# Which engine waits for the output store: GpSimd or ScalarE

## The chip, the cores and the metric

The kernel runs on one core of one Trainium2 chip. The profile of the core lists the instructions of TensorE (PE; PEld is its weight load), VectorE (DVE), ScalarE (ACT), GpSimd (POOL) and SyncE (SP), 10032 in all in the kernel before, and gives the DMA's time as a share of 16 engines. In this kernel the engines' programs meet through semaphores. The metric is the device time of one execution in microseconds (us), the median of several executions.

Two kinds of evidence are used:

- times of whole executions, which for one kernel in one set of rounds spread by 0.06 to 0.8 us;
- the trace's own records, to the nanosecond: the instructions, the updates of each semaphore, and the DMA packets. The semaphore records go on after the kernel's last instruction, in the kernel before from 0.122 to 2.269 us after the store's last increment, so they also show how the core leaves the program. All times "after the last increment" below are taken from these records; tables in plain fences were made from them.

The "span" is the time from the kernel's first instruction to its last in the profile; the reported time is longer (1287.31 against 1285.28 us in the profiled run of the kernel before), as it also holds what the core does on leaving.

## The reference, cut to what matters

The reference is one decode step for one token: attention over a cache of 32768 keys for 32 heads, plus a SwiGLU feed-forward block, plus the input. Its result is one row of 640 bfloat16 values.

```python
x = A_x
xn = _layernorm(x, axis=-1)
return x + _A_ref(xn, A_k_cache, A_v_cache, A_wq, A_wo) \
         + _B_ref(xn, B_w_gate, B_w_up, B_w_down)
```

The caches make the work: 554 MB come from HBM, 1280 bytes go back. Only the way those 1280 bytes are waited for is at issue here.

## The kernel before: the parts that matter

`nc.Block` gives each engine a program. SyncE issues all the large loads and, at the very end, the store of the result:

```python
@block.sync
def sp(e):
    ...                                   # all loads
    e.wait_ge(s_fin, 2)                   # VectorE has cast the output row
    e.dma_start(out[0, 0:1, :].rearrange("o (r m) -> (o r) m", m=32),
                orow[:, :]).then_inc(s_out, 16)
```

`then_inc(s_out, 16)` is the program's request that the store's completion raise the semaphore `s_out` to 16. In the trace of the kernel before, that semaphore has eleven records after the store's issue, from 0.498 to 1.259 us after it. An engine waits until it stands at 16; the wait is meant to keep the program from ending before the result has landed. Every version measured here has such a wait, and no run tests what happens without one. Before the change it is GpSimd, which otherwise only builds constants at the start (its last memset ends at 4.5 us):

```python
@block.gpsimd
def pool(g):
    def done(ins):
        ins.then_inc(s_const, 1)
        n[0] += 1
        g.wait_ge(s_const, n[0])
    ...                                   # identity matrices, masks
    for a in range(RB):
        done(g.memset(blk[a * 32:(a + 1) * 32, a:a + 1], 1.0))
    assert n[0] == 6 + 2 * RB
    g.wait_ge(s_out, 16)
```

ScalarE's last work lies well before the end (it ends at 1270.33 us):

```python
@block.scalar
def act(a):
    ...
    a.wait_ge(s_f, 1)
    a.activation(out=sg[:, 0, :], in_=ffn[:, 0:FB], func=ACTF.Exp, scale=-1.0).then_inc(s_fa, 1)
```

Two details of the surroundings matter. The kernel empties its last block (`nc.main_func.blocks[-1].instructions = []`), and its engines end one by one: in the changed kernel GpSimd's final branch starts at 4.5 us and ScalarE's at 1284.8 us. And in these traces a wait is carried by the instruction behind it. `done` leaves a wait for `s_const` pending after the last memset, and GpSimd's last two records in the kernel before are one instruction that only waits for `s_out` (17 ns), then a compare-and-branch that carries the wait for `s_const` (32 ns). The profile gives that branch the line of the `with` statement, L80. An engine with nothing pending shows no such branch: in the kernel before L80 has one record, GpSimd's, in the changed kernel two, GpSimd's and ScalarE's.

## Time and profile before

| | before |
|---|---|
| time, median of 3 runs (range) | 1286.85 us (1286.80 to 1286.95) |
| span of the profiled run | 1285.3 us |
| HBM traffic, rate | 554 MB, 431 GB/s |
| SyncE issues the output store | 1283.903 us |
| last completion increment of the store | 1285.162 us |
| GpSimd's final branch ends; the span ends with it | 1285.284 us |

Lines of the page of the kernel before: its span, the DMA share in 40 slices, and the main DMA queue.

```profile
span 1285.3 us, 10032 instructions
...
DMA  9999999999999999999999999999999999999998
...
q1 hardware_dynamic: 10974, 554.00, 99.7%
...
HBM read 553.99 MB, written 0.00 MB: 431 GB/s over the span
```

The DMA engines are at least 90% busy in every slice but the last, and the main queue's packets take 99.7% of the span at 431 GB/s: by these figures the kernel is bound by HBM traffic. The view by stretches of time shows where that stops. The columns are the stretch, its length, the busy time of each engine, the granted TensorE clock, the share of DMA and GB/s.

```profile
core 0: us, PE busy (x) PEld busy (x) DVE busy (x) ACT busy (x) POOL busy (x), PEclk, DMA share, GB/s
1252.00:1270.00 18.00, 17.63 (x413) 17.50 (x412) 2.52 (x6) 1.14 (x4) 0.00 (x0) 0.59 0.99 418
1270.00:1282.00 12.00, 6.20 (x207) 5.87 (x204) 0.96 (x5) 0.18 (x1) 0.00 (x0) 0.50 0.94 385
1282.00:1285.30 3.30, 1.39 (x37) 1.12 (x34) 0.36 (x2) 0.00 (x0) 0.00 (x0) 0.50 0.03 8
```

After 1282 us the DMA share is 0.03. These last 3.3 us are a chain of short instructions, each waiting for the one before, and, with a DMA share of 0.94 to 0.99 in the two stretches before, the one in which half a microsecond on GpSimd or ScalarE can count. The timeline of this stretch, before (start, length, engine, line, operation):

```profile
1283.22 0.18 DVE L641 TENSOR_TENSOR outb<-ps,blk 128x20 bf16<-128x20 f32 x1 [11.79 <-PE ps L451]
...
1283.46 0.20 PE L476 MATMUL ps<-fold,outb 128*20 128x32 bf16 x1 [0.27 <-DVE outb L641]
1283.70 0.18 DVE L644 CAST orow<-ps 20x32 bf16<-20x32 f32 x1 [0.29 <-PE ps L476]
1283.90 0.39 SPq L255 DMA_DIRECT2D out_dram<-orow  x1
```

The timeline ends with the store, but the span ends 1 us later: waits and branches are not drawn there. The view of single source lines shows them, first GpSimd's wait for the store:

```profile
L278 POOLq EVENT_SEMAPHORE  x1: 17/17/17, 1285.2 to 1285.2; - x1
```

and then the branch behind it:

```profile
L80 POOLq COMPARE_BRANCH  x1: 32/32/32, 1285.3 to 1285.3; - x1
```

Each line gives the count, the length in ns and the first and last start in us. In the trace they start at 1285.186 and 1285.252 us.

What happens then is in no view of the profile, only in the semaphore records. In the kernel before, semaphore 2 is raised step by step ("ticks"), nine times up to 1025 ns after the last increment. From 945 to 1591 ns 245 semaphores have one record each, in five groups by number of 47 to 50 (46 to 51 in the changed kernel), which I read as resets. From 1905 to 2269 ns nine more ticks follow. I read the first nine ticks as a barrier, and the last nine as a second one; no view names them. I call the first five ticks, one by each engine (the experiments with each engine in turn as the last show which is whose), the way out, and the next four the way back; a step from one tick to the next is a hop. The "exit" of an engine is the time from the end of its final branch to its own tick. In ns after the store's last increment:

```
                     barrier, way out              way back            last barrier
kernel before   -1326 -1292  747  791  814    906  944  978 1025    1905 ... 2269
                          ^ GpSimd's branch ended at 122
```

Two engines had long ticked. The third tick comes 747 - 122 = 625 ns after GpSimd's branch, and the rest follows.

### The profile page before, as it was taken

How to read it: one execution, taken by the hardware profiler on the slowest of the kernel's cores; microseconds unless marked ns; L12 is line 12 of the kernel's file. 1: busy time of each engine (PE TensorE's matmuls, PEld its weight loads, DVE VectorE, ACT ScalarE, POOL GpSimd, SP SyncE). 2: the span in 40 equal slices, each digit the busy share in tenths (PEclk: the TensorE clock that was granted, in tenths of full speed). 3: DMA queues.
4: the chain of work that ended last, by engine and by line, in shares of the span. 5: the costliest groups of instructions: out<-in, count | busy, mean ns of one | idle time of the engine just before them, and what ended most of it. 6: DMA issues, size and time to landing. Idle time of an engine off the chain costs nothing.

```text
span 1285.3 us, 10032 instructions
## 1 busy us (share of the span) xinstructions
PE 1041.2 (81%) x5160; PEld 261.3 (20%) x3240; DVE 672.3 (52%) x409; ACT 52.1 (4%) x139; POOL 2.6 (0%) x18
## 2 busy tenths in 40 slices
PE   3599777789788789778898877798787798778797
PEld 1022112221112221112221112221112221112227
DVE  0855665445665446664446664446654446654441
ACT  2000000000000000000000000000000000000000
POOL 0000000000000000000000000000000000000000
PEclk9799888898888898888998888898888998888995
DMA  9999999999999999999999999999999999999998
GB/s 424 424 447 429 428 437 435 428 432 439 432 432 432 439 428 432 439 432 432 428 443 428 432 439 432 432 426 445 428 432 439 430 434 426 441 432 432 439 419 364
DMA packets 10987, 554.16 MB, mean 431 GB/s; under 512 B 1247, under 2 KB 1504, under 8 KB 1760
## 3 DMA queue, kind: packets, MB, share of 16 engines
q1 hardware_dynamic: 10974, 554.00, 99.7%
q8 instruction: 9, 0.15, 0.0%
q14 instruction: 2, 0.02, 0.0%
q10 hardware_dynamic: 2, 0.00, 0.0%
HBM read 553.99 MB, written 0.00 MB: 431 GB/s over the span
## 4 chain that ended last, share of the span: by engine, by line
DMA 53%; PE 28%; DVE 12%; issue 6%; DVEq 0%; SPq 0%
DMA ring<-in_A_k_cache_dram 51%; PE ps L358 16%; DVE ring L577 12%; PE ps L310 9%; DMA ring<-in_A_wo_dram 2%; PE ps L342 1%; PE ps L329 1%; PE ps L400 0%; PE ps L394 0%; PE ps L388 0%; PE ps L451 0%; SPq L252 0%; DVEq L577 0%; DVE sc L583 0%; DVE pmax L589 0%
## 5 line engine op out<-in xcount | busy, mean ns | idle before, releaser
L577 DVE TENSOR_TENSOR ring<-ring,qb 128x8192 bf16<-128x8192 bf16 x128 | 557.8, 4421 | 315.8 <-DMA ring<-in_A_k_cache_dram 315.8
L310 PE MATMUL ps<-ring,ident 128*128 128x512 bf16 x1920 | 497.2, 418 | 0.0
L358 PE MATMUL ps<-ring,P 128*4 128x512 bf16 x1920 | 429.0, 379 | 0.0
L329 PE MATMUL ps<-ring,ident 128*128 128x512 bf16 x128 | 55.9, 437 | 220.1 <-DVE ring L577 219.8
L358 PEld LDWEIGHTS ps<-ring,P 128*4 128x4 bf16 x1920 | 158.1, 85 | 230.1
L329 PEld LDWEIGHTS ps<-ring,ident 128*128 128x128 bf16 x128 | 12.6, 98 | 617.6 <-issue 309.7
L583 DVE TENSOR_REDUCE sc<-ps 128x64 f32<-128x512 f32 x128 | 82.3, 686 | 62.8 <-PE ps L310 62.8
L595 DVE TENSOR_SCALAR negb<-ps 128x1 f32<-128x1 f32 x32 | 5.1, 159 | 108.4 <-PE ps L400 108.4
L503 ACT ACTIVATE P<-sc,negb 128x256 bf16<-128x256 f32 x32 | 16.2, 508 | 956.9 <-DVE negb L595 956.9
L592 DVE TENSOR_REDUCE m<-ps 1x1 f32<-1x128 f32 x32 | 8.9, 278 | 85.2 <-PE ps L394 85.2
L380 PEld LDWEIGHTS ps<-identf,o 4*128 4x128 f32 x248 | 30.7, 190 | 13.1 <-issue 13.1
L380 PE MATMUL ps<-identf,o 4*128 4x1 f32 x248 | 33.3, 251 | 0.0
L388 PEld LDWEIGHTS ps<-rsum,ones 128*128 128x128 f32 x64 | 12.1, 190 | 99.3 <-issue 98.5
L494 ACT ACTIVATE o<-ps,rzb 4x512 f32<-4x512 f32 x31 | 21.0, 677 | 6.3 <-PE ps L345 6.3
L301 PE MATMUL ps<-ring 128*128 x40 | 10.6, 432 | 11.2 <-DMA ring<-in_A_wq_dram 11.2
L499 ACT ACTIVATE ocol<-ps 128x1 f32 (+1 forms) x31 | 5.4, 173 | 222.4 <-PE ps L380 222.4
L342 PE MATMUL ps<-ring,P 128*4 x64 | 14.4, 379 | 0.0
L589 DVE TENSOR_REDUCE pmax<-sc 128x1 f32<-128x256 f32 x32 | 13.5, 421 | 0.0
L394 PE MATMUL ps<-identf,pmax 128*1 128x128 f32 x64 | 12.2, 272 | 1.2 <-DVE pmax L589 1.2
L400 PE MATMUL ps<-m,ones 1*128 1x1 f32 x64 | 12.1, 256 | 0.4 <-DVE m L592 0.4
L400 PEld LDWEIGHTS ps<-m,ones 1*128 1x128 f32 x64 | 9.4, 183 | 14.0 <-issue 13.3
L565 DVE RECIPROCAL rzb<-ps 128x1 f32<-128x1 f32 x32 | 5.1, 158 | 8.1 <-PE ps L388 8.1
(75 smaller groups left out, 97.3 us busy)
## 6 DMA issues: line engine op xcount, KB each, us to landing
ring<-in_A_v_cache_dram SPq DMA_DIRECT2D x2, 4096.0 KB, 36.5
ring<-in_A_wq_dram SPq DMA_DIRECT2D x1, 5120.0 KB, 15.5
ring<-in_A_wo_dram SPq DMA_DIRECT2D x3, 1280.0 KB, 24.6
ring<-in_B_w_gate_dram SPq DMA_DIRECT2D x1, 2160.0 KB, 22.6
ring<-in_B_w_up_dram SPq DMA_DIRECT2D x1, 2160.0 KB, 27.9
ring<-in_B_w_down_dram SPq DMA_DIRECT2D x1, 2080.0 KB, 31.0
ring<-in_A_wo_dram SPq DMA_DIRECT2D x1, 800.0 KB, 28.7
ring<-in_A_k_cache_dram SPq DMA_DIRECT2D x32, 41.4
```

The costliest lines, as they stand in the source:

```text
L310: return t.add_instruction(mybir.InstMatmult(start_tensor_calc=False, stop_tensor_calc=stop, tile_size=(128, 128), tile_position=(0, 0), l ...
L329: t.matmul(ob, lhsT=ident[:, :], rhs=src, start=True, stop=False)
L342: t.matmul(O, lhsT=P[:, h % PR, bass.ds(b * (RUN * W) + j, W)], rhs=flat[:, bass.ds(b * (RUN * W * DH) + (s * CE + j * DH), W * DH)], star ...
L358: mm = t.matmul(O, lhsT=P[:, h % PR, j:j + W], rhs=ring[:, s, j * DH:(j + W) * DH], start=(j == 0), stop=(j + W == NJ))
L380: mm = t.matmul(fold_ps, lhsT=o4[:, m * DH:(m + 1) * DH], rhs=identf[0:W, m:m + 1], start=(m == 0), stop=(m == W - 1))
L394: t.matmul(misc[0:1, 0:128], lhsT=pmax[:, h % SR:h % SR + 1], rhs=identf[:, :], start=True, stop=True).then_inc(s_t, 1)
L400: t.matmul(misc[:, 128:129], lhsT=ones[0:1, :], rhs=m1[0:1, h % SR:h % SR + 1], start=True, stop=True).then_inc(s_b, 1)
L494: a.activation(out=o4[:, :], in_=O, func=ACTF.Copy, scale=rzb[0:W, h % SR:h % SR + 1]).then_inc(s_o4, 1)
L503: a.activation(out=P[:, h % PR, :], in_=sc[:, :], func=ACTF.Exp, bias=negb[:, h % SR:h % SR + 1], scale=c_scale, accum_out=rsum[:, h % SR: ...
L577: v.tensor_tensor(out=kh, in0=kh, in1=q[:, None, :].to_broadcast([128, HF, DH]), op=ALU.mult).then_inc(s_mul, 1)
L583: v.tensor_reduce(out=sc[:, i * HF:(i + 1) * HF], in_=bank[i].rearrange("p (j e) -> p j e", e=G), axis=AX.X, op=ALU.add).then_inc(s_red, 1)
L589: v.tensor_reduce(out=pmax[:, h % SR:h % SR + 1], in_=sc[:, :], axis=AX.X, op=ALU.max).then_inc(s_max, 1)
```

## The change

The intent is to take the wait away from GpSimd and give it to ScalarE, which is idle by then as well. It is the whole diff:

```diff
@@ gpsimd
                 assert n[0] == 6 + 2 * RB
-                g.wait_ge(s_out, 16)
@@ scalar
                 a.activation(out=sg[:, 0, :], in_=ffn[:, 0:FB], func=ACTF.Exp, scale=-1.0).then_inc(s_fa, 1)
+                a.wait_ge(s_out, 16)
```

## The prediction

> **What bounds the kernel now.** HBM traffic. The page shows 554 MB moved in a span of 1285.3 us at 431 GB/s, with the DMA engines at 9 tenths in 39 of 40 slices and queue q1 busy for 99.7% of the span. Only the end is not DMA-bound: the windows view gives a DMA share of 0.03 from 1282.0 to 1285.3 us. The change touches only those last microseconds.
>
> **The end, from the timeline and the trace's semaphore records.** DVE casts orow at 1283.70 and SyncE issues the output store at 1283.90 (0.39 us). The store's completion semaphore gets its last increment at 1285.162. GpSimd, idle since 4.5 us, sees it at 1285.186 (its wait, L278, 17 ns), runs a final branch at 1285.252 (32 ns), and the span ends at 1285.284. ScalarE's last instruction (L527) ended at 1270.33.
>
> After the span comes the exit barrier, visible as ticks of semaphore 2: two engines had ticked at 1283.836 and 1283.870; the third tick, which I read as GpSimd's, came at 1285.909, 0.625 us after its branch; then ticks 44 and 23 ns apart, semaphore resets, and a last barrier to 1287.43. In that 0.625 us lies a DMA packet of kind "instruction" (8192 bytes, 1285.339, 474 ns). I read it as GpSimd fetching the code behind its program. [...] the trace shows the packet, not the stall.
>
> **What the change removes, adds, moves.** No DMA, matmul or arithmetic changes. One semaphore wait leaves GpSimd and appears on ScalarE. The store's 1.26 us from issue to last increment stays on the critical path entirely. Moved:
> 1. GpSimd reaches its branch and fetch near 4.5 us, hidden: up to 0.5 us off the end if the fetch is a stall, 0 if it is only a prefetch.
> 2. ScalarE is now the last to arrive. No instruction packet lies near 1270.3 us, when it finished before, so I expect none at the end. Its branch should absorb the wait (ScalarE's loop branches take 40 to 45 ns): about 0.05 us less than wait plus branch on GpSimd.
> 3. If ScalarE ticks one place before GpSimd, the barrier has one hop more on the path: about 0.04 us (ticks are 23 to 47 ns apart).
>
> Sum: a gain between 0 and 0.5 us; my middle is 0.2 us, 0.016% of the time. The wait stands behind ScalarE's last activation, so nothing earlier is delayed.
>
> **Predicted:** 1286.65 us, 80% range 1286.0 to 1287.3 (before's three runs spread by 0.15 us; the rest is for another session or chip). Chances: faster by over 2% 0.003, within 2% 0.994, slower by over 2% 0.003.
>
> **What would show each step right or wrong.** Page shares and GB/s should be unchanged. The span should still end about 0.05 to 0.1 us after the store's last increment, now with a ScalarE instruction. Step 1: the instruction packet after the span disappears, one appears near 5 us, and the gap from span end to the barrier's next tick falls from 0.625 to some 0.2 us. If the packet stays, ScalarE pays the same fetch and the gain is near zero. Step 3: one tick only, not two, stands before the gap.
>
> **What would make it wrong.** A fetch by ScalarE after its now real final branch; the 0.625 us being ordinary exit work that ScalarE has too, or has more of; a drift of the HBM rate, where 0.1% is already 1.3 us, larger than the effect.

## The result, and the profile after

| | before | after |
|---|---|---|
| time, median of 4 runs each (range) | 1286.90 us (1286.80 to 1286.96) | 1286.36 us (1286.32 to 1286.43) |
| ratio of the means | | 0.9996 (0.9979 to 1.0013) |
| profiled run | 1287.31 us | 1286.37 us |
| span of the profiled run | 1285.284 us | 1284.817 us |
| store: issue to last increment | 1.259 us | 1.263 us |
| last increment to end of the final branch | 0.122 us | 0.059 us |
| end of that branch to GpSimd's tick | 0.625 us | 0.237 us |

A ratio is the mean time of one kernel's fast runs over that of the other's of the same rounds, so not quite the ratio of the quoted medians. 0.54 us is 0.04%, and the interval allows for 0.1 to 0.2%. The four runs of one kernel nevertheless do not overlap with those of the other.

The page of the changed kernel has the same traffic at the same rate:

```profile
span 1284.8 us, 10032 instructions
...
DMA  9999999999999999999999999999999999999998
...
q1 hardware_dynamic: 10974, 554.00, 99.8%
...
HBM read 553.99 MB, written 0.00 MB: 431 GB/s over the span
```

The timeline of the last stretch, after, has the same four steps of the same lengths, each about 0.4 us earlier in this profile (line numbers on PE and ACT are one less):

```profile
1282.82 0.18 DVE L641 TENSOR_TENSOR outb<-ps,blk 128x20 bf16<-128x20 f32 x1 [11.30 <-PE ps L450]
...
1283.05 0.20 PE L475 MATMUL ps<-fold,outb 128*20 128x32 bf16 x1 [0.27 <-DVE outb L641]
1283.29 0.18 DVE L644 CAST orow<-ps 20x32 bf16<-20x32 f32 x1 [0.29 <-PE ps L475]
1283.49 0.39 SPq L255 DMA_DIRECT2D out_dram<-orow  x1
```

That 0.4 us was there before the store was issued, so before ScalarE's wait had anything to wait for. The chain of work that ended last shows it in the last weights, in the kernel before:

```profile
1252.98 28.71 DMA ring<-in_A_wo_dram
1281.69 0.05 issue
1281.73 1.47 PE ps L451 x40
```

and after:

```profile
1253.07 28.21 DMA ring<-in_A_wo_dram
1281.28 0.05 issue
1281.32 1.47 PE ps L450 x40
```

The last weights took 28.21 us to land in one profile and 28.71 us in the other. Over all profiles the store was issued anywhere from 1283.447 to 1283.903 us. The two profiles of the kernel before are the two latest (1283.643 and 1283.903 us), but the timed runs show no such difference: worked back from their spans, an estimate, the store was issued at 1283.6 us on average in 23 runs of the kernel before as in 13 of the changed kernel, 0.04 us apart. The profile of before was a late one (1287.31 us against a median of 1286.9). So the difference of the two profiled runs, 0.94 us, must not be read as the effect.

What the change did is in the lines of the final branches, after:

```profile
L80 POOLq COMPARE_BRANCH  x1: 33/33/33, 4.5 to 4.5; - x1
L80 ACTq COMPARE_BRANCH  x1: 38/38/38, 1284.8 to 1284.8; - x1
```

GpSimd now leaves at 4.5 us. On ScalarE no wait instruction of its own appears: its branch, 38 ns, carries the wait for `s_out`. The exit, in ns after the store's last increment:

```
                     barrier, way out              way back            last barrier
kernel before   -1326 -1292  747  791  814    906  944  978 1025    1905 ... 2269
kernel after    -1331   257  296  340  363    455  493  527  574    1364 ... 1729
```

Counted from the last increment, the last tick came 2269 - 1729 = 540 ns earlier. This is made of 63 ns up to the end of the final branch (122 to 59), 388 ns from there to the third tick (625 to 237), nothing up to the end of the way back (278 in both), and 89 ns from the end of the way back to the last tick. In all 13 profiles the reported time is the moment of the last tick less 0.109 to 0.122 us, so the reported time does end with those ticks, and a shorter exit is counted in full.

### The profile page after: what moved, and what is told of

Read it like the earlier page. It is cut to its first block, busy times and chain, and to the rows that moved or that the text cites. A ratio compares the mean times of both kernels' runs of the same rounds, so it can differ in the third digit from the quotient of the medians.

```text
span 1284.8 us, 10032 instructions
## 1 busy us (share of the span) xinstructions
PE 1044.1 (81%) x5160; PEld 261.3 (20%) x3240; DVE 672.2 (52%) x409; ACT 52.2 (4%) x139; POOL 2.6 (0%) x18
## 4 chain that ended last, share of the span: by engine, by line
DMA 53%; PE 28%; DVE 12%; issue 6%; DVEq 0%; SPq 0%
DMA ring<-in_A_k_cache_dram 51%; PE ps L357 16%; DVE ring L577 12%; PE ps L309 9%; DMA ring<-in_A_wo_dram 2%; PE ps L341 1%; PE ps L328 1%; PE ps L399 0%; PE ps L393 0%; PE ps L387 0%; PE ps L450 0%; SPq L252 0%; DVEq L577 0%; DVE sc L583 0%; DVE pmax L589 0%
```

## The experiments

Theory 1, after seeing the result: GpSimd needs about 0.62 us from its final branch to the barrier, whoever else does what; ScalarE needs 0.20 us. Whichever engine is released last by the store puts its own exit on the critical path. Rivals: the gain is a merit of ScalarE's wait rather than of GpSimd's absence; GpSimd's exit is slow because of its leftover wait; it is slow because GpSimd has slept for 1.28 ms; the stall on an instruction fetch, which the prediction had proposed.

All eleven runs gave correct results. "Gain" is the median of the kernel before less that of the experiment in the same rounds. A second, cleaner number is given with it: the time of each run less its span, which takes out whatever happened up to the end of the final branch (so also the 63 ns that the change saves there). The spans are listed to 0.1 us only, so it is used as a mean. Its mean for the kernel before was 2.01 us over 23 runs of these rounds.

### The changed kernel again: after_again

> The changed kernel once more, as a control on this chip. Every theory: about 0.5 us below the kernel before (286.3 against 286.9 in the last digits, so a gain between 0.4 and 0.65 us). In the trace: ScalarE's final branch ends 0.06 us after the store's last completion increment, the next tick of the exit barrier follows 0.20 us after that, and the last tick of the last barrier lies 1.73 us after the last increment (2.27 us in the kernel before).

Median 1286.45 us against 1286.92 us, a gain of 0.47 us. Last increment to branch end 60 ns, branch to tick 198 ns, last tick at 1729 ns, all within 2 ns of the first profile. Time less span was 1.57 us, 0.44 us less than before. The effect repeats.

### Both engines wait: both_wait

```diff
 # gpsimd: g.wait_ge(s_out, 16) stays
 # scalar, after the last activation
+                a.wait_ge(s_out, 16)
```

> ScalarE and GpSimd both wait for the store. Theory 1 (GpSimd's own way from its final branch to the barrier takes about 0.63 us whenever it is released, ScalarE's 0.20 us): the time goes back to that of the kernel before, within 0.1 us, with GpSimd's tick 0.75 us after the last increment. Theory 2 (the gain comes from something ScalarE's wait adds, for instance that ScalarE is awake when the barrier comes): the gain of about 0.5 us stays.

Median 1287.04 us against 1286.92 us: no gain (time less span 2.00 us). Both branches are in the profile:

```profile
L80 ACTq COMPARE_BRANCH  x1: 38/38/38, 1284.8 to 1284.8; - x1
L80 POOLq COMPARE_BRANCH  x1: 33/33/33, 1284.8 to 1284.8; - x1
```

```
both_wait       -1331   258  747  791  814    904  943  978 1024    1905 ... 2269
```

ScalarE's tick is at 258 ns as in the changed kernel, and the barrier then stands still until GpSimd's at 747 ns as in the kernel before. So ScalarE's wait brings nothing by itself, and the gain is GpSimd's absence from the end. The run also shows that the second tick is ScalarE's and the third GpSimd's.

### GpSimd waits, without the leftover wait: pool_branch

```diff
-                    done(g.memset(blk[a * 32:(a + 1) * 32, a:a + 1], 1.0))
+                    m = g.memset(blk[a * 32:(a + 1) * 32, a:a + 1], 1.0)
+                    if a < RB - 1:
+                        done(m)
+                    else:
+                        m.then_inc(s_const, 1)   # no wait behind the last one
+                        n[0] += 1
```

> GpSimd waits for the store as before, but its leftover wait for its last memset is dropped, so that the wait for the store rides on the final branch as it does on ScalarE in the changed kernel. Theory 1: the branch ends about 0.06 us after the last increment instead of 0.12, so the gain is about 0.06 us and the 0.63 us from the branch to the tick stays. Rival (the leftover wait or the separate wait instruction is what makes GpSimd's exit slow): the gap of 0.63 us falls to about 0.2 us and the gain is about 0.4 us or more.

Median 1286.79 us against 1286.92 us, a gain of 0.13 us. The branch, now carrying the wait for the store, ended 57 ns after the last increment instead of 122; the tick came at 676 ns, which is 619 ns after the branch. The form of the wait is worth 65 ns; the slow exit stays. The rest of the 0.13 us is of the size of the 90 ns that come and go (see `before_again`).

```
pool_branch     -1330 -1296  676  720  743    833  872  907  953    1745 ... 2110
```

This trace also speaks on the instruction packet that the prediction blamed: here it lasted from 171 to 720 ns, and GpSimd's tick at 676 ns did not wait for its end.

### GpSimd waits, woken shortly before: pool_warm

```diff
                 assert n[0] == 6 + 2 * RB
+                g.wait_ge(s_fin, 2)
+                done(g.memset(warm[:, :], 0.0))    # a scratch tile of its own
                 g.wait_ge(s_out, 16)
```

> GpSimd waits for the store as before, but 1.5 us earlier it is woken by the cast of the output row and does one small memset. Theory 1 (exit of GpSimd takes 0.63 us always): same time as before within 0.1 us, tick 0.75 us after the last increment. Rival (GpSimd is slow because it has slept for 1.28 ms, so that its code or its sequencer is cold): the gap from its branch to the tick falls to about 0.2 us and some 0.4 us are gained.

Median 1286.94 us against 1286.92 us: no gain. GpSimd ran its memset about 1.2 us before the last increment, and still took 737 - 118 = 619 ns from its branch to its tick. The long sleep is not the cause. (The memset shows that the engine was awake; it is no test of a fetch of code behind the program. For that see the packet in the account below.)

### ScalarE waits, GpSimd ends late: pool_late

```diff
 # on the changed kernel; gpsimd
                 assert n[0] == 6 + 2 * RB
+                g.wait_ge(s_fin, 2)
```

> The changed kernel (ScalarE waits for the store), but GpSimd ends late too: it waits for the cast of the output row, 1.47 us before the store's last increment. Theory 1 (GpSimd's exit of 0.62 us only costs where it runs after the store's completion): GpSimd is ready for the barrier some 0.6 us before the last increment, so the time is that of the changed kernel, within 0.1 us, and ScalarE's tick lies 0.26 us after the last increment and the next 0.04 us behind it. Rival (GpSimd has to be done long before the end, or any late end of GpSimd costs the 0.4 us): back to the time of the kernel before, or in between.

Median 1286.51 us against 1287.04 us, a gain of 0.53 us.

```profile
L80 POOLq COMPARE_BRANCH  x1: 33/33/33, 1283.6 to 1283.6; - x1
L80 ACTq COMPARE_BRANCH  x1: 37/37/37, 1284.9 to 1284.9; - x1
```

GpSimd's branch ended 1.16 us before the last increment. Its tick followed ScalarE's by the usual 39 ns (257 and 296), so it was ready and waiting. The exit of GpSimd costs nothing once it lies under the store's latency; it does not have to be at the start of the kernel.

### SyncE waits: sp_wait

```diff
 # on the kernel before; gpsimd
-                g.wait_ge(s_out, 16)
 # sync, behind the store
+                e.wait_ge(s_out, 16)
```

> SyncE, which issues the store, waits for it; ScalarE and GpSimd do not. Theory 1 with an exit like ScalarE's (0.20 us from branch to tick) and with SyncE last in the order of ticks: its tick 0.26 us after the last increment with no hop behind it, where the changed kernel has its last first-round tick at 0.363 us; so 0.10 us below the changed kernel, 0.6 us below the kernel before. If SyncE's exit is slow as GpSimd's, the tick comes at 0.68 us and 0.3 us are lost against the changed kernel. Rival (the gain was ScalarE's alone): the time of the kernel before.

Median 1286.48 us against 1287.04 us, a gain of 0.56 us; time less span 1.43 us, 0.15 us less than the changed kernel's 1.57 us. It was run at another time.

```profile
L80 POOLq COMPARE_BRANCH  x1: 33/33/33, 4.5 to 4.5; - x1
L80 SPq COMPARE_BRANCH  x1: 33/33/33, 1284.9 to 1284.9; - x1
```

```
kernel after    -1331   257   296   340  363    455  493  527  574    1364 ... 1729
sp_wait         -1272 -1238 -1200 -1140  268    312  350  385  432    1224 ... 1588
```

SyncE's branch ended at 50 ns and its tick came at 268 ns, an exit of 218 ns. All four other ticks stand before the last increment, so SyncE is the last in the order and no hop lies behind it. The way back is 48 ns shorter at its first step too (44 instead of 92), which I had not expected. A reading that fits, but that no run isolates: the first engine of the way back is VectorE, and here its own tick lay 1.4 us before SyncE's instead of 23 ns.

### VectorE waits: dve_wait

```diff
 # on the kernel before; gpsimd
-                g.wait_ge(s_out, 16)
 # vector, behind the cast of the output row
+                v.wait_ge(s_out, 16)
```

> VectorE waits for the store. Theory 1 with an exit of 0.20 to 0.25 us and VectorE last but one in the order: its tick 0.26 to 0.31 us after the last increment, the next 0.023 us later, so 0.03 to 0.08 us below the changed kernel, some 0.55 us below the kernel before. Rival (the gain was ScalarE's alone): the time of the kernel before.

Median 1286.66 us against 1287.04 us, a gain of 0.38 us. VectorE's branch ended at 75 ns, its tick came at 339 ns: an exit of 264 ns, the longest but GpSimd's. The way back ended at 580 ns against 574 ns in the changed kernel. My expectation of 0.03 to 0.08 us below the changed kernel was a miss: the two saved hops (83 ns) were eaten by the longer exit (264 against 198 ns) and the later end of the branch (75 against 59 ns).

### TensorE waits: pe_wait

```diff
 # on the kernel before; gpsimd
-                g.wait_ge(s_out, 16)
 # tensor, behind its last matmul
+                t.wait_ge(s_out, 16)
```

> TensorE waits for the store. Theory 1 with TensorE first in the order of ticks: four hops (0.034, 0.038, 0.044, 0.023 us) stand behind its tick, so with ScalarE's exit of 0.20 us the first round ends 0.40 us after the last increment, 0.03 us later than in the changed kernel; 0.5 us below the kernel before. Both ticks that stand before the last increment in the kernel before now come after it. Rival (the gain was ScalarE's alone): the time of the kernel before.

Median 1286.90 us against 1287.04 us, a gain of 0.14 us. From the last increment to the end of the way back the trace has 754 ns against 1025 ns before, 0.27 us less.

```profile
L80 PEldq COMPARE_BRANCH  x1: 179/179/179, 1284.8 to 1284.8; - x1
```

The exit behind the branch is short (403 - 208 = 195 ns), but the branch alone takes 179 ns, where ScalarE's takes 38. With four hops behind it the way out ended at 543 ns, not at the 400 ns that I had expected. The direction was right, the size was missed by that branch. The trace of the kernel before could have warned: TensorE's loop branches there (L299) take 76 to 231 ns. All five ticks lie after the last increment: TensorE is the first in the order.

### The two best side by side: after_third and sp_wait_again

> The changed kernel beside the version in which SyncE waits, on one chip, five rounds. Theory 1: about 0.5 us below the kernel before; last tick 1.73 us after the store's last increment.

> SyncE waits for the store. The trace of the first such run has the last tick of the exit 1.588 us after the store's last increment against 1.729 us in the changed kernel. Theory 1 (the time ends with those ticks): 0.14 us below the changed kernel of the same rounds and 0.6 to 0.7 us below the kernel before. Rival (the first run's medians, 1286.48 and 1286.45 us in different rounds, mean what they say): no gain over the changed kernel.

| five runs each | median (range) | mean | time less span, mean |
|---|---|---|---|
| kernel before (9 runs) | 1286.95 us (1286.74 to 1287.46) | 1286.99 us | 1.99 us |
| ScalarE waits | 1286.58 us (1286.27 to 1287.06) | 1286.59 us | 1.61 us |
| SyncE waits | 1286.33 us (1286.26 to 1286.79) | 1286.41 us | 1.49 us |

The whole times are noisier (ratios 0.9997 and 0.9996). Two expectations on the traces were missed: the last tick came at 1818 ns (ScalarE) and 1671 ns (SyncE) instead of 1729 and 1588 ns, both by the 90 ns of the next section. ScalarE's gain in the medians is 0.37 us here, where about 0.5 us was expected. The last column repeats: SyncE's version leaves 0.12 us sooner than ScalarE's here, and the end of the way back lay at 431 ns against 573 ns. So a version that beats both kernels exists, by a little over 0.1 us in the records; the whole times agree in direction and are too noisy to settle it alone.

### The kernel before again: before_again

> The kernel before, profiled once more. Theory 1: GpSimd's tick 0.75 us after the last increment, 0.625 us after its branch. Open: between the last semaphore reset of the engine that ticks first and its next tick lay 0.314 us in the first profile and in both_wait, but 0.224 us in all other runs, pool_warm among them. If 0.314 us comes again, it belongs to this kernel's exit; if 0.224 us, it varies from run to run and is no part of what the change does.

One look, 1287.04 us. GpSimd's tick came at 747 ns, 625 ns after its branch. By the measure named in the expectation the answer is 0.224 us, so no part of what the change does; and 0.314 us came instead in `after_third`, a profile of the changed kernel. But that measure misses some of it: in `before_again` and `sp_wait_again` the last group of resets began 306 to 308 ns after the end of the way back instead of 217 to 219 ns. So I took the whole stretch. From the end of the way back (1024 ns) to the next tick it took 874 ns. Over all 13 profiles this stretch is either 784 to 792 ns (eight profiles) or 874 to 881 ns (five). The changed kernel itself has 790, 791 and 881 ns, the version with SyncE 792 and 876. So these 90 ns come and go with the same program. They are part of the 540 ns between the first two traces, and I do not count them as an effect of the change. Both profiles of the kernel before had the long value, the second in a call in which all three profiles had it. Whether that is more than chance stays open, but time less span points that way. From the traces it should be 1.94 us for the kernel before with the short value and 2.03 us with the long one, and its mean over 23 runs was 2.01 us; for the changed kernel 1.55 and 1.64 us, and its mean over 13 runs was 1.58 us. By this estimate the long value is commoner in the kernel before and is worth some 0.04 us of the gain in whole times. No run shows why.

## Why the prediction was right or wrong

The end of the way back leaves those 90 ns out, and is the best single account (ns):

```
who waits            branch ends   its tick   exit   way back ends
GpSimd (before)          122          747      625       1025
GpSimd, merged wait       57          676      619        953
GpSimd, woken            118          737      619       1014
GpSimd and ScalarE       123          747      624       1024
ScalarE (after)           59          257      198        574
VectorE                   75          339      264        580
TensorE                  208          403      195        754
SyncE                     50          268      218        432
```

All are counted from the last increment, except the exit (in the row with both engines, GpSimd's numbers).

The order on the way out in these runs is TensorE, ScalarE, GpSimd, VectorE, SyncE, with hops of 34 to 35, 38 to 39, 43 to 44 and 23 to 24 ns where no exit lay in the hop (in `sp_wait` the hop to VectorE took 60 ns); that the way back is the reverse is read from the hops, not isolated. The nine ticks of the last barrier took 364 to 365 ns from first to last. The final branch, where it carries the wait for the store, took 33 ns on SyncE and GpSimd, 37 to 38 on ScalarE, 47 on VectorE and 179 on TensorE.

- **The bound and the size of the stake: right.** Nothing outside the last microseconds moved, the rate stayed at 431 GB/s, and the store still takes 1.26 us.
- **The time: right in the range, off in the middle.** Predicted was 1286.65 us, a gain of 0.2 us on 1286.85; measured 1286.36 us, a gain of 0.54 us on 1286.90. The range reached from 1286.0 to 1287.3 us and so held the time of the kernel before as well: that the measured time lies in it says nothing of the mechanism. The part that the records tie to the change is 1025 - 574 = 451 ns, inside the predicted "between 0 and 0.5 us" and near its upper end.
- **Step 1: the wrong step.** The prediction read the 8192-byte instruction packet as "GpSimd fetching the code behind its program", and made the gain depend on whether that fetch was a stall or a prefetch. It wrote: "If the packet stays, ScalarE pays the same fetch and the gain is near zero." The packet stayed, and the gain came. One of its signs came true for another reason, which was luck: the gap fell to "some 0.2 us" (0.237). The packet did not appear near 5 us, when GpSimd now leaves. In the changed kernel it starts 171 ns after the last increment and lasts 324 ns, so it was still under way when ScalarE's tick (257 ns) and all the others of the way out had passed. In every profile it starts 152 to 190 ns after the last increment, whoever waits. It is therefore not tied to GpSimd's branch, and it did not hold up the way out: even where GpSimd waited, in `pool_branch`, the tick came at 676 ns and the packet ended at 720. The trace of the kernel before already spoke against the reading: two more such packets on the same queue lie at 115.4 and 1256.8 us, while GpSimd stood waiting from 4.5 us on. Which engine fetches it is open. So is what times it: the store's issue and its last increment are 1.256 to 1.267 us apart in all 13 profiles, so the records can't tell these two apart. That such a fetch could stall the engine was the author's assumption and was not shown: the packet lasts from 177 to 651 ns in the kernel before, no other instruction packet lies in these 625 ns, and no trace shows a stall in them.
- **What step 1 should have said.** The prediction's own last paragraph had it as what could go wrong: "the 0.625 us being ordinary exit work that ScalarE has too, or has more of". It behaves like that, a time that GpSimd takes on its way out whenever it is released last, and ScalarE's is shorter: 198 ns against 619 to 625 ns in five profiles with GpSimd waiting. So the term was mis-sized: the gain could be 0 in the sum only if both engines had an equal exit, for which no number of the profile of before spoke; the difference measured 427 ns.
- **Step 2: right.** ScalarE's branch absorbs the wait: 122 ns become 59, a saving of 63 ns where "about 0.05 us" was predicted. On GpSimd the same merging gave 65 ns.
- **Step 3: right.** ScalarE stands one place before GpSimd, so one hop more is on the path: 39 ns, where "about 0.04 us" was predicted, and one tick instead of two stands before the gap.

The sum: 625 - 198 = 427 ns from the exit, plus 63 ns from the merged wait, less 39 ns for the hop, is 451 ns.

What GpSimd does in its 0.62 us is not settled. It lies behind the final branch, the last instruction in the trace of the kernel before, and leaves no record. Shown is that it is not the long sleep (619 ns in `pool_warm`), not the leftover wait (619 ns in `pool_branch`) and not a wait for the end of that packet (in `pool_branch` the tick came at 676 ns, the end at 720), and that it is hidden when GpSimd's branch ends 1.16 us before the store's last increment (`pool_late`) or at 4.5 us (the changed kernel).

## What to carry to other kernels

In this kernel each engine had its own way out of the program (195 to 625 ns), and the reported time ended with the last tick behind it, less 0.109 to 0.122 us. So look for an engine with a short exit and a late place in the exit barrier to be released last; here that was SyncE (the way back ended at 432 ns), then ScalarE (574 ns), never GpSimd (953 to 1025 ns). GpSimd's slow exit cost nothing once it lay under the store's latency of 1.26 us (`pool_late`, still a gain of 0.53 us), so let such an engine end early. No other kernel was measured. And before a packet that happens to lie inside a gap is called its cause, ask whether it is tied to the gap's owner: its other occurrences in the same trace, and its distance to other events in a second kernel, would have told.
